# A transposed down-projection, six row buffers and a ScalarE copy in the last stage of an attention and gated-MLP kernel

## The chip, the cores and the metric

The kernel runs on one core of one Trainium2 chip. The time is the device time of that core in microseconds, as the median of several runs. The engines named here are PE (TensorE, matrix products), ACT (ScalarE, activations), DVE (VectorE), POOL (GpSimd) and SP (SyncE, which issues nearly all DMA transfers). Each engine works through its own queue of instructions in a fixed order, written out by the program when it is built.

## The reference

The input `x` has 2048 rows of 640 columns. It is normalized, and two branches read the result: attention with 32 heads of 20 columns, and a gated MLP of width 1728. Their results are combined.

```python
xn = _layernorm(x, axis=-1)
# A: q, k, v = xn @ wqkv, 32 heads of 20
scores = jnp.einsum("bhqd,bhkd->bhqk", q, k) * scale
p = _softmax(scores, axis=-1)
o = jnp.einsum("bhqk,bhkd->bhqd", p, v)
s = o @ wo
# B
h = _sigmoid(xn @ w_gate) * (xn @ w_up)
g = _silu(h @ w_down)
return x + s * g
```

## The kernel before

**Blocks.** The 32 heads form 8 groups of 4, and the 2048 queries form 4 chunks of 512, so there are 32 blocks (group, chunk). A block has 64 score tiles (4 heads by 16 tiles of 128 keys), each of 128 keys by 512 queries: 2048 in all. PE computes a score tile into a bank of PSUM. Two double banks, `scA0` and `scA1`, take two tiles each; three spare banks, `bk0` to `bk2`, take single tiles and the results of all other products. The four heads of a group occupy four strips of 32 rows of the array, so several score tiles run side by side (L900).

**Exponentials.** ScalarE takes most tiles out as exps, two at a time from a double bank (`pt<-scA`, 1024 columns) or one from a spare bank (`px<-bk`, 512 columns). The others go to VectorE, which makes an integer with the bits of a rough power of two (`iv`, L1336) and improves it in three passes over four tiles (`pb`, L1030, L1033, L1036). PE multiplies the results with `v` into one bank, `oacc` (L937). After each block VectorE copies `oacc` out (`norm_a`), and the denominators go through DRAM and back: SP stores `ld`, loads `lt`, VectorE takes reciprocals (`norm_b`), SP stores `rd` and loads `rl`, GpSimd multiplies, and SP puts the heads into `oU`.

**The MLP** fills PE between the scores. For each chunk of 512 rows there are 14 tiles of 128 columns of gate and up (`mk_gu`): ScalarE takes a tanh, VectorE a product, and `hT` holds the result with the MLP's columns on the partitions. Then comes the down-projection (`mk_down`): eight items per chunk, one for each 128 rows and each half of the 640 output columns, with 14 steps of four matmuls 320 columns wide. `hT` is the stationary operand, so rows come out on the partitions. ScalarE takes a tanh of 320 columns (`td`), VectorE a product (`gqs`), and SP stores it in `gq_dram` in fp32. The last chunk's product stays in SBUF (`gql`).

**Output.** Near the end `mk_out` multiplies `oU` with `wo` for each 128 rows and half of the columns, VectorE multiplies with the row of `gq_dram` that `load_out` has read back (`otmp`, L796), and GpSimd (L805) or, from row tile 8 on, VectorE (L814) adds `x`. Row buffers lie in the no longer needed part of `xnT`: three of them.

**The last stage** (`chain`, L1135 on) handles the last block and the last four row tiles. Most of their output products are formed early (`early`, L1057). When the last exp is multiplied, `oacc` is copied out in halves, transposed by PE, scaled and transposed back (`e_on` to `e_o`); `e_late` adds the last products (L1061). Four results of 512 columns (`mains`) lie in `bk0`, `bk1` and the halves of `scA1`; the last 128 columns of the four tiles lie in two banks (`rest`). VectorE multiplies them with `gql` (`t_main` L1107, `t_rest` L1113); GpSimd adds `x` for the first two tiles (L1110, L1117), VectorE for the last two (L1117, L1121); `t_out` stores.

**The order** of PE, ACT, DVE and POOL is written by a planner, the loop at the end of the kernel. It advances a clock in steps of 0.02 us with an assumed duration for every instruction and picks, for each engine that is free, the next work. PE chooses between score tiles (F), products with `v` (PV) and other items (M). Other items are held to a pace, at most `LEAD` us ahead of it; `M_ORD`, `DORD` and `XORD` set in which order the spare banks are tried for items, for VectorE's tiles and for ScalarE's extra tiles. GpSimd adds are placed by `beat` beside a VectorE instruction that reads PSUM, or all at once by `flush`. SP's order follows from when the planner's clock reaches each transfer.

Of the kernel before, what the change touches and what calls it, by code (L numbers as in the profile page):

```python
# [18 lines left out]
P = 128  # L19
# [11 lines left out]
URGENT, ROUNDS, HOLD, SLACK, LEAD, LAG, D_LAST, D_LAST_END = 0.2, 6, 0.0, 0.0, 40.0, 2.0, 20, 20  # L31
M_ORD, WAIT3, FALL, M_END = 1, 0.2, 1, 2.0
NPT, NPX, NPB, NIV = 12, 5, 3, 3
DVE_ADD = 8
XMAX, DQ, DORD, XORD, STARVE = 2, 1.4, 2, 0, 0.3
# [17 lines left out]
def kernel(  # L53
# [41 lines left out]
    gq_dram = dram.tile([S, D], FP32, name="gq_dram", tag="gqd", bufs=1)  # L95
# [352 lines left out]
    LATE, T_LT, T_OU, T_L2, T_RL = 1.0, 9.0, 1.5, 4.5, 5.6  # L448
# [216 lines left out]
    def mk_gu(c, kf, at):  # L665
# [20 lines left out]
        def th():  # L686
            st["t"] = w2.tile([P, QC], BF16, tag="tnh", bufs=2, name="tnh")
            act_imm(st["t"][0:fs, :], st["g"][0:fs, :], ACT.Tanh, 0.5)
# [8 lines left out]
        def th2():  # L697
            st["t"] = w2.tile([P, QC], BF16, tag="tnh", bufs=2, name="tnh")
            act_imm(st["t"][fs:P, :], st["g"][0:fs, :], ACT.Tanh, 0.5)
# [14 lines left out]
    def gq_last(t4):  # L714
        if len(gq_l) == t4 // 2:
            w = w2.tile([P, 2, KD, 2 * P], BF16, tag="wgu", bufs=2, name="gql")
            gq_l.append(w.rearrange("p i k f -> p (i k f)").bitcast(FP32))
        return gq_l[t4 // 2][:, t4 % 2 * D:(t4 % 2 + 1) * D]

    def mk_down(c, t4, h, at):  # L720
        st = {}
        tt = 4 * c + t4
# [4 lines left out]
        def mm(kf):  # L727
            cols(st["ps"][:, 0:HD], hT[:, kf, t4 * P:(t4 + 1) * P], wd[:, kf, h * HD:(h + 1) * HD],
                 kf == 0, kf == NFT - 1)

        def th():
            st["td"] = w2.tile([P, HD], BF16, tag="td", bufs=2, name="td")
            act_imm(st["td"], st["ps"][:, 0:HD], ACT.Tanh, 0.25)

        def ev():
            if c == NQC - 1:
                return nc.vector.scalar_tensor_tensor(out=gq_last(t4)[:, h * HD:(h + 1) * HD], in0=st["td"], scalar=1.0,
                                                      in1=st["ps"][:, 0:HD], op0=ALU.add, op1=ALU.mult)
            flush("o")
            gqs = w2.tile([P, HD], FP32, tag="gqs", bufs=3, name="gqs")  # L740
            ins = nc.vector.scalar_tensor_tensor(out=gqs, in0=st["td"], scalar=1.0, in1=st["ps"][:, 0:HD],
                                                 op0=ALU.add, op1=ALU.mult)
            nc.sync.dma_start(out=gq_dram[tt * P:(tt + 1) * P, h * HD:(h + 1) * HD], in_=gqs)
            return ins
        return Item([("PE", alloc, [(0.14, lambda kf=kf: mm(kf)) for kf in range(NFT)]),
                     ("ACT", 0.32, th), ("DVE", 0.40, ev, "free", mark("d", c, t4, h))], at, pre=[("h", c, kf) for kf in range(NFT)])
# [17 lines left out]

    def load_out(tt):
        if tt in out_tiles:
            return
        o2 = xfl[:, tt % 3 * KD * QC:tt % 3 * KD * QC + 3 * D]
        flush("o")
        out_tiles[tt] = (o2[:, 0:D], o2[:, D:3 * D].bitcast(FP32))  # L770
# [3 lines left out]
    def mk_out(tt, h, at):  # L774
        st = {}

        def alloc():
            if h == 0:
                load_out(tt)
                if (tt + 1) % 4:  # L780
                    load_out(tt + 1)
# [6 lines left out]
        def ev():  # L788
# [6 lines left out]
            tmp = w2.tile([P, 2 * HD], BF16, tag="gqs", bufs=3, name="otmp")[:, 0:HD]  # L795
# [16 lines left out]
        def add():  # L812
            xr = out_tiles[tt][0][:, h * HD:(h + 1) * HD]
            ins = nc.vector.tensor_tensor(out=xr, in0=st["tmp"], in1=xr, op=ALU.add)  # L814
            if h == 1:
# [4 lines left out]
                    pre=[("d", tt // 4, t4, i) for t4 in range(4) for i in range(2)] + [("h", 2, kf) for kf in range(NFT)] + (  # L820
# [4 lines left out]
    for c in range(NQC):  # L825
        for kf in range(NFT):
            glu.append(lambda at, c=c, kf=kf: mk_gu(c, kf, at))
        for h in range(2):
            for t4 in range(4):
                glu.append(lambda at, c=c, t4=t4, h=h: [mk_down(c, t4, h, at)])  # L830
# [271 lines left out]
    tmps = [hfl[:, t4 * 512:(t4 + 1) * 512] for t4 in range(4)]  # L1102
    tmp = hfl[:, 4 * 512:4 * 512 + 4 * EX].rearrange("p (t e) -> p t e", e=EX)
    xg = xl.rearrange("p (t u) -> p t u", u=D)

    def t_main(t4):
        nc.vector.scalar_tensor_tensor(out=tmps[t4], in0=mains[t4], scalar=0.25, in1=gq_last(t4)[:, 0:512],  # L1107
                                       op0=ALU.mult, op1=ALU.mult)
        if t4 < 2:
            nc.gpsimd.tensor_tensor(out=tail[t4][:, 0:512], in0=tmps[t4], in1=tail[t4][:, 0:512], op=ALU.add)  # L1110

    def t_rest(i):
        nc.vector.scalar_tensor_tensor(out=tmp[:, 2 * i:2 * i + 2, :],  # L1113
                                       in0=rest[i][:, 0:2 * EX].rearrange("p (t e) -> p t e", e=EX),
                                       scalar=0.25, in1=gq_l[i].rearrange("p (t u) -> p t u", u=D)[:, :, 512:D],
                                       op0=ALU.mult, op1=ALU.mult)
        (nc.vector if i else nc.gpsimd).tensor_tensor(out=xg[:, 2 * i:2 * i + 2, 512:D], in0=tmp[:, 2 * i:2 * i + 2, :],  # L1117
                                                      in1=xg[:, 2 * i:2 * i + 2, 512:D], op=ALU.add)

    def t_last(t4):  # L1120
        nc.vector.tensor_tensor(out=tail[t4][:, 0:512], in0=tmps[t4], in1=tail[t4][:, 0:512], op=ALU.add)  # L1121

    def t_out(t4):
        r = slice(4 * (NQC - 1) * P + t4 * P, 4 * (NQC - 1) * P + (t4 + 1) * P)
        eng = nc.sync if t4 % 2 == 0 else nc.scalar
        eng.dma_start(out=out2[r, :], in_=tail[t4])

    def t_done(i):
        t_rest(i)
        for t4 in (2 * i, 2 * i + 1):  # L1130
            if i:
                t_last(t4)
# [8 lines left out]
             ("DVE", 0.63, lambda: t_main(0), (10,)), ("DVE", 0.63, lambda: t_main(1), (10,)),  # L1141
# [397 lines left out]
```

## Time and profile before

| | us |
|---|---|
| median of 3 runs (801.88 to 803.19) | 802.37 |
| the profiled execution, its own time | 803.29 |
| its span, first to last instruction | 801.6 |

| engine | busy, us | share of the span | instructions |
|---|---|---|---|
| PE | 779.8 | 97% | 10465 |
| ACT | 781.8 | 98% | 992 |
| DVE | 770.1 | 96% | 1246 |
| POOL | 96.4 | 12% | 203 |

| group | count | mean of one, ns |
|---|---|---|
| ACT exp of two tiles, `pt` | 703 | 1192 |
| ACT exp of one tile, `px` | 137 | 762 |
| ACT tanh of the down-projection, `td` | 32 | 618 |
| DVE `iv` | 499 | 683 |
| DVE product of the down-projection, `gqs` and `gql` | 32 | 483, 475 |
| PE down-projection matmuls, 128x320 | 1792 | 302 |

The mean of one counts from an instruction's start to its end. Neighbours overlap on an engine, so what an instruction costs its engine is the distance to the next start, where the next one is ready. The DMA engines are busy for about a quarter of the time.

### The profile page before, as it was taken

The numbers are of one execution on the slowest core, as the hardware profiler recorded it, in microseconds if no ns is written. First come the engines' busy times: TensorE is split into PE (matmuls) and PEld (weight loads), VectorE is DVE, ScalarE is ACT, GpSimd is POOL, SyncE is SP. The second block draws the span as 40 slices with busy tenths as digits, with TensorE's granted clock in tenths as the row PEclk, the third lists the DMA queues.
The fourth block names the chain that finished last, engine by engine and source line by source line (L and its number), as shares of the span: only waits on it lengthen the run. The fifth ranks groups of instructions, "written<-read, shape, count | busy, mean of one in ns | idle before, by whom it ended". The sixth has DMA issues, their size and how long they took to land.

```text
span 801.6 us, 25384 instructions
## 1 busy us (share of the span) xinstructions
PE 779.8 (97%) x10465; PEld 284.4 (35%) x10465; DVE 770.1 (96%) x1246; ACT 781.8 (98%) x992; POOL 96.4 (12%) x203
## 2 busy tenths in 40 slices
PE   8899999999999999999999999999999999999997
PEld 5523333333433323334332332333333233333332
DVE  7798999999999999989999999999999999999997
ACT  8799999999999999999999999999999999999994
POOL 7200000000000000000000000000000100502302
PEclk9999999999999999999999999999999999999999
DMA  5441212223122223222113232222311332331421
GB/s 162 132 131 49 69 40 73 66 67 81 47 62 67 73 72 100 53 60 65 53 46 89 58 87 73 73 81 62 98 36 61 91 89 53 102 107 23 141 70 55
DMA packets 91851, 60.47 MB, mean 75 GB/s; under 512 B 34891, under 2 KB 85627, under 8 KB 91735
## 3 DMA queue, kind: packets, MB, share of 16 engines
q1 hardware_dynamic: 91447, 58.52, 26.1%
q8 instruction: 82, 1.34, 0.7%
q14 instruction: 34, 0.28, 0.1%
q10 hardware_dynamic: 288, 0.33, 0.1%
HBM read 45.18 MB, written 11.09 MB: 70 GB/s over the span
## 4 chain that ended last, share of the span: by engine, by line
PE 45%; ACT 41%; DVE 7%; issue 5%; DMA 1%; SPq 0%; POOL 0%; DVEq 0%; ACTq 0%; POOLq 0%
ACT pt L83 33%; PE bk L474 18%; PE scA L900 14%; PE oacc L937 9%; ACT px L83 4%; DVE iv L1336 2%; ACT tnh L83 2%; DVE pb L1036 1%; ACT td L83 1%; PE bk L900 1%; DVE pb L1033 1%; PE tp L293 1%; DVE pb L1030 0%; DMA lt<-ld 0%; DMA ld<-on 0%
## 5 line engine op out<-in xcount | busy, mean ns | idle before, releaser
L83 ACT ACTIVATE pt<-scA 128x1024 bf16<-128x1024 f32 (+1 forms) x709 | 708.7, 1188 | 0.7 <-PE bk L900 0.3
L1336 DVE TENSOR_SCALAR iv<-bk 128x512 int16<-128x512 f32 x499 | 332.2, 683 | 12.1 <-PE bk L900 9.6
L900 PE MATMUL scA<-q,kT 32*128 32x512 bf16 x1412 | 275.8, 382 | 8.8 <-ACT pt L83 3.3
L900 PE MATMUL bk<-q,kT 32*128 32x512 bf16 x636 | 207.3, 383 | 0.2 <-DVE iv L1336 0.2
L900 PEld LDWEIGHTS <-kT 32*128 32x128 bf16 x2048 | 88.4, 91 | 262.4 <-issue 251.1
L937 PE MATMUL oacc<-pt,v 128*21 128x512 bf16 x1412 | 178.5, 381 | 0.7 <-ACT pt L83 0.7
L937 PE MATMUL oacc<-pb,v 128*21 128x512 bf16 x998 | 160.8, 382 | 0.0
L474 PE MATMUL bk<-xnT,wgu 128*32 128x512 bf16 x2160 | 157.3, 383 | 0.5 <-DVE iv L1336 0.2
L1036 DVE TENSOR_TENSOR pb<-iv,pb 128x2048 bf16<-128x2048 bf16 (+1 forms) x125 | 151.8, 1214 | 0.7
L990 POOL TENSOR_TENSOR on_bf<-on,rl 128x128 bf16<-128x128 f32 x116 | 54.3, 472 | 626.8 <-DVE iv L1336 189.1
L83 ACT ACTIVATE px<-bk 128x512 bf16<-128x512 f32 x137 | 102.1, 762 | 1.7 <-POOL hT L1178 1.6
L474 PE MATMUL bk<-wd,hT 128*32 128x320 bf16 x1792 | 87.0, 302 | 0.1
L1030 DVE TENSOR_SCALAR pb<-iv 128x2048 int16<-128x2048 int16 (+1 forms) x125 | 86.0, 688 | 0.4
L1033 DVE TENSOR_SCALAR pb<-iv 128x2048 int16<-128x2048 int16 (+1 forms) x125 | 85.9, 688 | 0.0
L937 PEld LDWEIGHTS <-v 128*21 128x21 bf16 x2547 | 53.6, 91 | 76.2 <-issue 53.6
L474 PEld LDWEIGHTS <-wgu 128*32 128x32 bf16 x2160 | 44.5, 95 | 64.3 <-issue 46.3
L474 PEld LDWEIGHTS <-hT 128*32 128x32 bf16 x1792 | 37.5, 95 | 38.2 <-issue 32.7
L474 PE MATMUL bk<-xnT,wu 128*32 128x512 bf16 x640 | 48.5, 383 | 0.6 <-DVE iv L1336 0.2
L937 PE MATMUL oacc<-px,v 128*21 128x512 bf16 x137 | 47.0, 381 | 0.0
L83 ACT ACTIVATE tnh<-bk 128x512 bf16<-128x512 f32 (+1 forms) x56 | 43.4, 776 | 0.1
L691 DVE SCALAR_TENSOR_TENSOR hT<-tnh,bk 128x512 bf16<-128x512 bf16 x52 | 35.4, 680 | 1.0 <-PE bk L900 0.3
L655 PE MATMUL bk<-wv,xnT 128*128 128x160 bf16 x280 | 29.4, 235 | 0.6 <-ACT px L83 0.6
(120 smaller groups left out, 406.2 us busy)
## 6 DMA issues: line engine op xcount, KB each, us to landing
rl<-rd SPq DMA_DIRECT2D x124, 64.0 KB
wgu<-in_B_w_gate_dram SPq DMA_DIRECT2D x24, 320.0 KB
wgu<-in_B_w_up_dram SPq DMA_DIRECT2D x24, 320.0 KB
gq_dram<-gqs SPq DMA_DIRECT2D x24, 160.0 KB
xnT<-gq_dram SPq DMA_DIRECT2D x12, 320.0 KB
xt<-in_A_x_dram SPq DMA_DIRECT2D x16, 160.0 KB
xnT<-in_A_x_dram SPq DMA_DIRECT2D x16, 160.0 KB
out_dram<-xnT SPq DMA_DIRECT2D x14, 160.0 KB
```

The lines of the kernel that those rows point to most:

```text
L83: return nc.scalar.add_instruction(mybir.InstActivation(func=func, name=nc.get_next_instruction_name(), engine=ENG.Activation, ins=[nc.sca ...
L293: nc.tensor.transpose(out=tps[k][:, kd, :], in_=xns[k][:, kd * P:(kd + 1) * P], identity=ident)
L474: nc.tensor.matmul(out[j:j + 32, :], lhsT=lhsT[:, j:j + 32], rhs=rhs, start=start, stop=stop, tile_position=(0, j), skip_group_check=True)
L655: nc.tensor.matmul(st["ps"][:, i * 2 * GC:(i + 1) * 2 * GC], lhsT=xn_tok(tts[i], kd), rhs=wvs[pr][:, kd, :], start=(kd == 0), stop=(kd == ...
L691: return nc.vector.scalar_tensor_tensor(out=hT[0:fs, kf, :], in0=st["t"][0:fs, :], scalar=1.0, in1=st["u"][0:fs, :], op0=ALU.add, op1=ALU. ...
L900: nc.tensor.matmul(dst, lhsT=kTs[gc_of(b)[0] % 2][32 * j:32 * j + 32, kt * P:(kt + 1) * P], rhs=qts[b % 3][32 * j:32 * j + 32, :], start=T ...
L937: nc.tensor.matmul(oacc[32 * j:32 * j + DH + 1, :], lhsT=lhsT, rhs=u["src"], start=first, stop=last, tile_position=(0, 32 * j), skip_group ...
L990: ins = nc.gpsimd.tensor_tensor(out=on_bf[:, cs], in0=on[:, cs], in1=rl[:, cs], op=ALU.mult)
L1030: ins = nc.vector.tensor_scalar(out=pb[:, 0, :, :].bitcast(I16), in0=iv, scalar1=0x7F80, scalar2=1, op0=ALU.bitwise_and, op1=ALU.bitwise_or)
L1033: ins = nc.vector.tensor_scalar(out=pb[:, 1, :, :].bitcast(I16), in0=iv, scalar1=0x007F, scalar2=0x3F00, op0=ALU.bitwise_and, op1=ALU.bitw ...
L1036: ins = nc.vector.tensor_tensor(out=pb[:, 1, :, :], in0=iv.bitcast(BF16), in1=pb[:, 1, :, :], op=ALU.mult)
L1336: beat(nc.vector.tensor_scalar(out=d["iv"][:, j, :], in0=bank[bk], scalar1=B_OFF, scalar2=0.0, op0=ALU.add, op1=ALU.max))
```

## The change

The down-projection swaps its operands. `wd` becomes the stationary one and `hT` the moving one, so an item is one tile of 128 output columns for all 512 rows of the chunk: five items per chunk, matmuls 512 wide. Output columns now lie on the partitions, so SP transposes each product with a DMA into `g4`, and a second transfer stores that in `gq_dram`, which is now bf16. For the last chunk the transpose writes straight into `gql`. `gqs` and `g4` have one buffer each. The planner issues the transpose 0.8 us after VectorE's product starts (`T_GT`) and the store 5.8 us after it (`T_GO`).

With bf16 rows, six row buffers fit where three were, and `load_out` is called up to `AHEAD` = 4 row tiles ahead.

In the last stage ScalarE copies one bank of each half out of PSUM, scaled by 0.25 (`t_copy`), and VectorE's product for these two banks reads SBUF alone. The add of the first half's last 128 columns moves from GpSimd to VectorE. VectorE adds each of the last two tiles in one instruction of 640 columns. Three of the four stores go through SP.

Four of the planner's settings change too: `LEAD` from 40 to 30, `M_ORD` from 1 to 0, `DORD` from 2 to 0 and `XORD` from 0 to 1. The tanh buffers become three and are shared with the down-projection.

```diff
-URGENT, ROUNDS, HOLD, SLACK, LEAD, LAG, D_LAST, D_LAST_END = 0.2, 6, 0.0, 0.0, 40.0, 2.0, 20, 20
-M_ORD, WAIT3, FALL, M_END = 1, 0.2, 1, 2.0
+URGENT, ROUNDS, HOLD, SLACK, LEAD, LAG, D_LAST, D_LAST_END = 0.2, 6, 0.0, 0.0, 30.0, 2.0, 20, 20
+M_ORD, WAIT3, FALL, M_END = 0, 0.2, 1, 2.0
...
-XMAX, DQ, DORD, XORD, STARVE = 2, 1.4, 2, 0, 0.3
+AHEAD = 4
+XMAX, DQ, DORD, XORD, STARVE = 2, 1.4, 0, 1, 0.3
...
-    gq_dram = dram.tile([S, D], FP32, name="gq_dram", tag="gqd", bufs=1)
+    gq_dram = dram.tile([S, D], BF16, name="gq_dram", tag="gqd", bufs=1)
...
-    def mk_down(c, t4, h, at):
+    def mk_down(c, e, at):
...
-            cols(st["ps"][:, 0:HD], hT[:, kf, t4 * P:(t4 + 1) * P], wd[:, kf, h * HD:(h + 1) * HD],
-                 kf == 0, kf == NFT - 1)
+            cols(st["ps"], wd[:, kf, e * P:(e + 1) * P], hT[:, kf, :], kf == 0, kf == NFT - 1)
...
-            st["td"] = w2.tile([P, HD], BF16, tag="td", bufs=2, name="td")
-            act_imm(st["td"], st["ps"][:, 0:HD], ACT.Tanh, 0.25)
+            st["td"] = w2.tile([P, QC], BF16, tag="tnh", bufs=3, name="td")
+            act_imm(st["td"], st["ps"], ACT.Tanh, 0.25)
...
-            nc.sync.dma_start(out=gq_dram[tt * P:(tt + 1) * P, h * HD:(h + 1) * HD], in_=gqs)
+            es = slice(e * P, (e + 1) * P)
+            g4 = w2.tile([P, 4, P], BF16, tag="g4", bufs=1, name="g4") if c < NQC - 1 else gq_last()[:, :, es]
+            timed.append((now + T_GT, lambda: nc.sync.dma_start_transpose(out=g4, in_=gqs)))
+            if c < NQC - 1:
+                timed.append((now + T_GO, lambda: nc.sync.dma_start(
+                    out=gq_dram[c * QC:(c + 1) * QC, es].rearrange("(t p) u -> p t u", p=P), in_=g4)))
...
-        o2 = xfl[:, tt % 3 * KD * QC:tt % 3 * KD * QC + 3 * D]
+        o2 = xfl[:, tt % 6 * 2 * D:(tt % 6 + 1) * 2 * D]
...
-            if h == 0:
-                load_out(tt)
-                if (tt + 1) % 4:
-                    load_out(tt + 1)
+            load_out(tt)
+            n = len(out_tiles)
+            if n < NOUT and n <= tt + AHEAD and (n < 6 or ("o", n - 6, 1) in ev_at) and all(
+                    ("d", n // 4, i) in ev_at for i in range(KD)):
+                load_out(n)
...
+    def t_add(eng, t4, a, b):
+        eng.tensor_tensor(out=tail[t4][:, a:b], in0=tmp[:, t4, a:b], in1=tail[t4][:, a:b], op=ALU.add)
+
+    def t_copy(t4):
+        act_imm(tmp[:, t4, 0:512], mains[t4], ACT.Copy, 0.25)
+
     def t_main(t4):
-        nc.vector.scalar_tensor_tensor(out=tmps[t4], in0=mains[t4], scalar=0.25, in1=gq_last(t4)[:, 0:512],
+        if t4 % 2:
+            nc.vector.tensor_tensor(out=tmp[:, t4, 0:512], in0=tmp[:, t4, 0:512], in1=gq_last()[:, t4, 0:512], op=ALU.mult)
+        else:
+            nc.vector.scalar_tensor_tensor(out=tmp[:, t4, 0:512], in0=mains[t4], scalar=0.25, in1=gq_last()[:, t4, 0:512],
+                                           op0=ALU.mult, op1=ALU.mult)
+        if t4 < 2:
+            t_add(nc.gpsimd, t4, 0, 512)
...
+        if not i:
+            nc.vector.tensor_tensor(out=xg[:, 0:2, 512:D], in0=tmp[:, 0:2, 512:D], in1=xg[:, 0:2, 512:D], op=ALU.add)
...
-        eng = nc.sync if t4 % 2 == 0 else nc.scalar
+        eng = nc.sync if t4 < 3 else nc.scalar
...
             if i:
-                t_last(t4)
+                t_add(nc.vector, t4, 0, D)
             t_out(t4)
```

## The prediction, made before the result was known

> **What bounds the kernel now.** The busy shares come first: PE 97%, DVE 96% and ACT 98% of the span, so the page alone does not say which of the three sets the pace. The profile cut into stretches of time does.
>
> ```profile
> 100.00:300.00 200.00, 197.32 (x2656) 68.05 (x2654) 197.39 (x316) 199.89 (x251) 16.32 (x36) 1.00 0.24 65
> 300.00:500.00 200.00, 196.90 (x2651) 68.20 (x2652) 194.18 (x304) 199.89 (x252) 14.39 (x32) 1.00 0.25 68
> 500.00:700.00 200.00, 197.07 (x2698) 70.47 (x2691) 197.63 (x311) 199.76 (x247) 24.02 (x48) 1.00 0.26 73
> 786.00:801.60 15.60, 9.93 (x81) 4.22 (x77) 9.62 (x21) 4.57 (x8) 2.88 (x3) 0.92 0.19 67
> ```
>
> The columns are PE, its weight loads, DVE, ACT and POOL. From 100 to 700 us ScalarE is busy for 599.5 of 600 us, PE for 591.3 and DVE for 589.2: ScalarE leads, with the other two close. Only after 786 us does it stand idle. Its timeline then shows what one instruction costs when the next follows at once.
>
> ```profile
> 399.07 3.99 ACT L83 ACTIVATE pt<-scA 128x1024 bf16<-128x1024 f32 x4
> 402.70 0.69 ACT L83 ACTIVATE td<-bk 128x320 bf16<-128x320 f32 x1
> 403.02 6.79 ACT L83 ACTIVATE pt<-scA 128x1024 bf16<-128x1024 f32 x7
> 409.43 0.71 ACT L83 ACTIVATE td<-bk 128x320 bf16<-128x320 f32 x1
> ```
>
> A 128x320 tanh takes 0.69 us but holds the engine for 0.32 (402.70 to 403.02). Seven exps of 1024 columns take 6.41, or 0.92 each. Over all starts from 40 to 786 us, a 1024-column exp has a median distance of 0.904 to the next start, and a 512-column one 0.477. What lies above these values is ScalarE waiting for scores under cover of its own latency, which "busy" hides: 13.0 us in 693 such exps. So 13 us is about all that a smoother order could win in the middle.
>
> The end is the other place. The timeline of the last 20 us:
>
> ```profile
> 781.27 1.85 POOL L995 TENSOR_TENSOR on_bf<-on,rl 128x512 bf16<-128x512 f32 x1 [18.24 <-DMA rl<-rd]
> 781.90 1.40 DVE L814 TENSOR_TENSOR xnT<-otmp,xnT 128x320 bf16<-128x320 bf16 x1
> ...
> 793.80 1.29 DVE L1107 SCALAR_TENSOR_TENSOR hT<-bk,gql 128x512 bf16<-128x512 f32 x2 [0.55 <-PE bk L1061]
> ...
> 794.64 2.26 POOL L1110 TENSOR_TENSOR xnT<-hT,xnT 128x512 bf16<-128x512 bf16 x2 [11.52 <-DVE hT L1107]
> ...
> 795.01 0.41 DVE L1113 SCALAR_TENSOR_TENSOR hT<-bk,gql 128x256 bf16<-128x256 f32 x1
> ...
> 795.42 1.29 DVE L1107 SCALAR_TENSOR_TENSOR hT<-scA,gql 128x512 bf16<-128x512 f32 x2
> ...
> 796.86 0.66 POOL L1117 TENSOR_TENSOR xnT<-hT,xnT 128x256 bf16<-128x256 bf16 x1
> 797.08 0.59 DVE L1117 TENSOR_TENSOR xnT<-hT,xnT 128x256 bf16<-128x256 bf16 x1
> ```
>
> VectorE works without a gap from 793.80 to 798.34 (the end of the last adds, L1121), then the last rows go out. And two pairs of these lines show VectorE and GpSimd excluding each other. The L814 add starts at 781.90 while GpSimd is at work until 783.12, and ends at 783.30: 1.40 us, against a median of 0.316 for its line. The L1117 add ends at 797.67, 0.15 us after GpSimd's 797.52. But the L1107 products, whose first input lies in PSUM, keep their 0.68 us right beside GpSimd's L1110. So a VectorE tensor_tensor on two SBUF inputs waits for a running GpSimd add; a product that reads PSUM does not.
>
> **The change, part by part.**
>
> *ScalarE's work.* From the two instruction orders: 32 tanhs of 320 columns become 20 of 512 (-32x0.317 + 20x0.477 = -0.60 us); two-bank exps 703 to 701 (-1.81), one-bank exps of a spare bank 137 to 140 (+1.43), half-filled exps 6 to 7 (+0.48). VectorE still takes 499 of the 2048 score tiles. Sum: **-0.5 us**, all on the engine that bounds.
>
> *PE and VectorE.* Down-projection streams 448 groups of 320 columns at 0.136 us before and 280 of 512 at 0.216 after: 60.9 against 60.5. Runs of it between score fills fall from 135 to 114; each entry and return costs some 0.10 us over the bare stream (0.32 against 0.216), so PE gains about 2 us. VectorE: -32x0.397 + 20x0.597 = -0.8. Neither bounds the middle; taken as nothing, and the cover is ScalarE's 599.5 of 600 us.
>
> *The order.* LEAD, the bank choices and the longer items rearrange PE from the first block on. What matters is how much PE work stands between two score fills against the exps that must bridge it. I price each stretch by the rows above (0.216 per 512-column stream, 0.21 for leaving and returning to scores) and subtract ScalarE's work of the same fill. In the trace of before, stretches where PE has over 0.15 us more than ScalarE cost ScalarE 0.07 us each on average, those within 0.05 cost 0.01. There are 111 such stretches before and 124 after; by that count the stalls go from 14.5 to 15.0 us (this count takes in the first exps). But they also follow one another more often: runs of four with over 0.2 us too much go from 36 to 57, and a straight-line fit of the measured stalls on single stretches and on runs of two and three gives 17.2. So +0.5 to +2.7; I take the middle, **+1.6 us**, as the two counts are equally near to the rows. The far bounds: all stretches at the quiet 0.01 (709x0.010 = 7 us) is -7.5; twice today's stalls is +14.5.
>
> *Transposes, stores, buffers.* SP issues 20 transposes and 15 stores for 24 stores, 11 more at 0.33 to 0.4 us; they stand between the loads of softmax denominators, weights and q. A store behind a transpose holds SP until it lands. No row has a transpose. Nearest is a round trip over DRAM: ld issued 397.62, lt (waiting for it) 399.35, 1.7 us. There is one gqs buffer, so VectorE's next product waits until the transpose has read it, with all later VectorE work queued behind. By ScalarE's order two tanhs are at least 6.9 us apart (7.3 to 11.4 mostly), which leaves 6.2 after the product's 0.7. So: nothing, unless a transpose takes over 6.2 us. [...] Loading rows ahead removes 9.0 us in which SP waited for otmp and 7.8 for output stores, but L796, the reader of those rows, has 0.0 us of idle before it: nothing.
>
> *Between last exp and end stage.* Before, the last exp ends at 789.83 and VectorE's first copy starts at 790.91, 1.08 later, as PE still has rows of oacc and early products to do. The new order leaves five PV matmuls, some 0.7 us: **-0.35** (0 to -0.4).
>
> *The end stage.* ScalarE's copy starts at 794.02 (its matmul ends at 793.98) and takes some 0.58 (the 512-column L174 from idle: 575 ns), to 794.60. The new SBUF product of bank 1 can start near 794.64, exactly when GpSimd's first add starts (794.638). If GpSimd is first, the product waits to 795.79 and ends at 796.06; GpSimd's second add runs 796.2 to 797.35; the add that moved from GpSimd to VectorE waits for it, to 797.5; then 0.61 (bank 2), 0.41 (bank 3), 0.33 (rest) and two adds of some 0.43 end at 799.7: +1.35. If VectorE is first, GpSimd runs 795.06 to 796.15 and 796.15 to 797.26, holds the moved add and the bank 3 product, and the end is 798.8: +0.45. Without any exclusion it is 797.9: -0.4. I take **+0.9**, the middle of the two with exclusion, which both pairs of rows show. [...]
>
> **Sum:** -0.54 + 1.6 - 0.35 + 0.9 = +1.6 us. The profiled execution took 803.29 us (span 801.57 and 1.72 around it), 0.92 above the median 802.37. So 804.9 against its own time and **804.0** against the median.
>
> **Rivals.**
> 1. *The new order stalls ScalarE less* (ends faster). Longer items change banks less often and free PE 2 us; if that counts more than the bunching, the stalls fall halfway to the quiet value, -3.75, and the sum is -3.7: 798.6. For it: PE shrinks. Against: stretches and runs over the limit grow. The other terms sum to 0.0, so it decides once the 13.0 us of waiting fall below 11.4 (-1.6).
> 2. *No exclusion in the end stage*, stalls +0.5: -0.54 + 0.5 - 0.35 - 0.4 = -0.8: 801.6. Against it stand L814 and L1117.
> 3. *Transposes are slow.* At 9 us the twenty products wait 13.9 us in all (each gap short of 9.7 us added up); if half reaches the end, +7 on the forecast: 811. Against: 1.7 us for a plain round trip.
>
> **How the numbers follow.** Some 0.2% (1.6 us) is what a measurement can tell from no change. Forecast 0.50 (its own range, with both ends of the stall and end-stage terms, 802.4 to 805.5), rival 1 0.26, rival 2 0.10, rival 3 0.14. The forecast lies at the 0.2% bound, and its stall term is open upwards: of its 0.50 I give 0.29 to slower and 0.21 to same. Faster: 0.24 of rival 1 and 0.01 of rival 2, 0.25; same: 0.21 + 0.02 + 0.09 = 0.32; slower: 0.29 + 0.14 = 0.43. The range leaves out the lower half of rival 1 and the slow end of rival 3: 799.0 to 808.5.
>
> **What would show it.** ScalarE's distances above 0.904 should sum to 13.5 to 16 us from 40 to 786. In the end stage the product of bank 1 or the moved add should last over 0.8 us beside a GpSimd add, and the last VectorE add should end 4.9 to 5.9 us after the first product's start (4.54 before). The product into gqs should start without waiting for a DMA. The prediction is wrong if the stalls fall under 11.4 us, if these adds keep 0.3 to 0.5 us, or if VectorE waits for transposes.

## The result, and the profile after

| | kernel before | changed kernel |
|---|---|---|
| median of 6 runs, us | 802.37 (801.88 to 803.24) | 805.72 (804.65 to 806.05) |
| ratio, with its 95% interval | | 1.0037 (1.0027 to 1.0047) |
| the profiled execution, us | 803.29 | 806.05 |
| its span, us | 801.57 | 804.35 |

The changed kernel is slower by 0.27 to 0.47%, more than the 0.2% that a measurement can tell from no change. The time lies in the predicted range, 1.7 us above the forecast and 0.2 above the 802.4 to 805.5 that the prediction gave for its own terms.

The spans of the two profiles can be compared piece by piece. "Work" counts each activation from the first exp on at the undisturbed distance of its form (0.904, 0.477, 0.317 us); "stalls" are what lies above it.

| piece | before | after | difference |
|---|---|---|---|
| start to first exp | 30.98 | 30.04 | -0.94 |
| ScalarE's work, first exp to start of last exp | 743.44 | 742.51 | -0.93 |
| stalls before 700 us | 12.33 | 12.65 | +0.32 |
| stalls from 700 us on | 2.33 | 5.20 | +2.87 |
| the last exp | 0.76 | 1.15 | +0.39 |
| its end to VectorE's first copy | 1.07 | 0.74 | -0.33 |
| copy to the first product of the last stage | 2.89 | 3.02 | +0.13 |
| first product to the end of VectorE's last add | 4.54 | 5.90 | +1.36 |
| the rest | 3.23 | 3.14 | -0.09 |
| sum | 801.57 | 804.35 | +2.78 |

The first row goes with PE's clock at the start, not with a stage of the change. In nine of the thirteen profiles of this document the trace's record of the full clock begins at 4.2 to 6.0 us (with one stretch of 3.4 us at 0.50 behind it), and the first exp comes at 29.9 to 30.3. In the other four (before, and experiments 6, 8 and 9) it begins at 13.8 to 14.1; up to there the 128x256 filler matmuls (`scrap`) last 0.42 us instead of 0.27, and the first exp comes at 30.8 to 31.0. Two of these four have the changed code, so the code alone does not set it; whether the kernel before can also start early, no profile shows. Two rows make the loss: the stalls from 700 us on, and the last stage.

The profile of the changed kernel cut into the same stretches (PE, its weight loads, DVE, ACT, POOL, then the granted clock):

```profile
100.00:300.00 200.00, 196.50 (x2496) 63.69 (x2488) 198.48 (x314) 199.95 (x247) 18.54 (x36) 1.00 0.25 65
300.00:500.00 200.00, 195.99 (x2510) 64.05 (x2510) 196.48 (x306) 199.86 (x251) 15.25 (x32) 1.00 0.27 70
500.00:700.00 200.00, 197.12 (x2515) 64.34 (x2511) 194.64 (x304) 199.80 (x245) 22.13 (x45) 1.00 0.28 73
788.30:804.40 16.10, 8.36 (x64) 3.70 (x63) 8.12 (x16) 5.18 (x8) 2.30 (x2) 0.89 0.12 45
```

From 100 to 700 us ScalarE leads as before, 599.6 of 600 us. So the middle is not where the time went.

**The event at 730 us.** The timeline of SP's queue (start, duration, transfer) in the changed kernel, and then the same transfers of the same block in the kernel before:

```profile
724.89 0.76 SPq L1022 DMA_DIRECT2D oU<-on_bf  x1
725.76 1.23 SPq L740 DMA_TRANSPOSE gql<-gqs  x1
727.04 0.75 SPq L1022 DMA_DIRECT2D oU<-on_bf  x1
727.89 0.53 SPq L974 DMA_DIRECT2D ld<-on  x1
728.48 1.50 SPq L1022 DMA_DIRECT2D oU<-on_bf  x2
730.08 0.42 SPq L976 DMA_DIRECT2D lt<-ld  x1
```

```profile
723.98 2.27 SPq L1020 DMA_DIRECT2D oU<-on_bf  x3
726.36 0.53 SPq L972 DMA_DIRECT2D ld<-on  x1
726.93 0.73 SPq L1020 DMA_DIRECT2D oU<-on_bf  x1
728.06 0.35 SPq L974 DMA_DIRECT2D lt<-ld  x1
```

`norm_a` issues the store `ld` and the load `lt` one after the other, yet transfers to `oU` stand between them on SP: the order on SP is not simply that in which the planner's clock reaches each transfer, as the description of the kernel before has it. In the changed kernel a transpose stands ahead of `ld` and holds the queue for 1.23 us, and two transfers instead of one stand between `ld` and `lt`. VectorE's copy (L972), whose result `ld` stores, came only 0.16 us later than before (723.54 against 723.38), but `lt` is issued 2.02 us later. Of these, 0.91 are there before the first transfer shown: GpSimd's four multiplies of the previous block, which release the `oU` transfers, end at 724.86 instead of 723.96. The other 1.11 are on the queue: from the first of the four `oU` transfers to `lt` it takes 5.19 us with the transpose among them, and took 4.08 without. So the transpose makes about half of the delay, and the new order of the engines the rest. Now VectorE, then ScalarE, in the changed kernel (start, duration, what ended the idle time before):

```profile
723.54 0.68 DVE L972 COPY on<-oacc 128x512 f32<-128x512 f32 x1
...
727.80 1.28 DVE L1345 TENSOR_SCALAR iv<-bk 128x512 int16<-128x512 f32 x2
731.77 0.25 DVE L982 RECIPROCAL rt<-lt 128x16 f32<-128x16 f32 x1 [2.69 <-DMA lt<-ld]
...
733.75 0.68 DVE L1345 TENSOR_SCALAR iv<-bk 128x512 int16<-128x512 f32 x1
```

```profile
736.17 1.02 ACT L84 ACTIVATE pt<-scA 128x1024 bf16<-128x1024 f32 x1 [2.00 <-PE bk L902]
737.69 1.02 ACT L84 ACTIVATE pt<-scA 128x1024 bf16<-128x1024 f32 x1 [0.49 <-PE bk L902]
739.20 2.07 ACT L84 ACTIVATE pt<-scA 128x1024 bf16<-128x1024 f32 x2 [0.48 <-PE bk L902]
```

VectorE stands 2.69 us in front of its reciprocal. In the kernel before it had stood 0.79 at this place, and 0.66 one block later:

```profile
729.62 0.25 DVE L980 RECIPROCAL rt<-lt 128x16 f32<-128x16 f32 x1 [0.79 <-DMA lt<-ld]
...
753.64 0.25 DVE L980 RECIPROCAL rt<-lt 128x16 f32<-128x16 f32 x1 [0.66 <-DMA lt<-ld]
```

Behind the reciprocal in the changed kernel's queue, after two passes over `pb`, is the `iv` that empties a spare bank; PE, whose next matmul needs that bank, stands for 2.19 us; and ScalarE runs out of scores. The stretches around it show a second loss:

```profile
732.00:734.40 2.40, 0.29 (x3) 0.09 (x1) 2.37 (x5) 2.17 (x3) 0.00 (x0) 1.00 0.04 3
734.40:736.90 2.50, 2.41 (x31) 0.71 (x30) 2.47 (x6) 0.73 (x1) 0.00 (x0) 0.82 0.45 136
736.90:739.70 2.80, 2.80 (x26) 0.47 (x22) 1.88 (x4) 1.82 (x3) 0.00 (x0) 0.55 0.18 25
```

After the gap PE's granted clock falls to half: in slices of 0.2 us it is 0.53 at 736.0 and 0.50 from 736.2 to 739.4, some 3.4 us in all, and score matmuls there last 0.61 us instead of 0.39. The two shorter waits of ScalarE, 0.49 and 0.48, lie there. The three waits make 2.97 us. Counted by the distance of starts, as in the table, they are 2.41, 0.61 and 0.60 us, together 3.62 against 0.36 at this place before: the whole rise of 2.87 from 700 us on, and more.

**The last stage** of the changed kernel, VectorE, GpSimd and ScalarE in order of time:

```profile
795.31 0.69 DVE L1117 SCALAR_TENSOR_TENSOR hT<-bk,gql 128x512 bf16<-128x512 f32 x1 [0.62 <-PE bk L1063]
...
796.14 1.15 POOL L1108 TENSOR_TENSOR xnT<-hT,xnT 128x512 bf16<-128x512 bf16 x1 [12.22 <-ACT hT L84]
796.16 1.42 DVE L1115 TENSOR_TENSOR hT<-hT,gql 128x512 bf16<-128x512 bf16 x1 [0.15 <-ACT hT L84]
...
797.72 1.15 POOL L1108 TENSOR_TENSOR xnT<-hT,xnT 128x512 bf16<-128x512 bf16 x1 [0.42 <-DVE hT L1115]
797.94 1.07 DVE L1128 TENSOR_TENSOR xnT<-hT,xnT 128x256 bf16<-128x256 bf16 x1
...
799.54 0.41 DVE L1115 TENSOR_TENSOR hT<-hT,gql 128x512 bf16<-128x512 bf16 x1
```

GpSimd starts 0.02 us ahead of VectorE's product of two SBUF inputs, and that product ends 0.29 us after GpSimd's add; the same product without GpSimd beside it takes 0.41. The moved add (L1128) again lasts until GpSimd is done: it ends at 799.01, GpSimd's second add at 798.87.

### The profile page after: what moved, and what is told of

It is laid out like the page before. It is cut to its first block, busy times and chain, and to the rows that moved or that the text cites. A ratio compares the mean times of both kernels' runs of the same rounds, so it can differ in the third digit from the quotient of the medians.

```text
span 804.3 us, 24012 instructions
## 1 busy us (share of the span) xinstructions
PE 773.9 (96%) x9788; PEld 263.5 (33%) x9793; DVE 770.0 (96%) x1234; ACT 782.7 (97%) x984; POOL 100.0 (12%) x202
## 4 chain that ended last, share of the span: by engine, by line
ACT 54%; PE 21%; DVE 14%; issue 9%; DMA 1%; SPq 1%; POOL 0%; DVEq 0%; ACTq 0%; POOLq 0%
ACT pt L84 43%; PE bk L475 8%; PE scA L902 6%; ACT px L84 6%; DVE iv L1345 6%; PE oacc L939 4%; ACT tnh L84 3%; DVE pb L1038 2%; DVE pb L1032 1%; DVE pb L1035 1%; ACT td L84 1%; DVE hT L692 1%; PE tp L294 1%; DMA xt<-in_A_x_dram 0%; PE psk L144 0%
## 5 line engine op out<-in xcount | busy, mean ns | idle before, releaser
L84 ACT ACTIVATE pt<-scA 128x1024 bf16<-128x1024 f32 x708 | 698.8, 1162 | 3.4 <-PE bk L902 3.0
L902 PE MATMUL bk<-q,kT 32*128 32x512 bf16 x639 | 203.1, 384 | 0.2
L939 PE MATMUL oacc<-pt,v 128*21 128x512 bf16 x1409 | 185.4, 382 | 0.9 <-ACT pt L84 0.8
L902 PEld LDWEIGHTS <-kT 32*128 32x128 bf16 x2048 | 85.9, 91 | 289.2 <-issue 279.1
L475 PE MATMUL bk<-xnT,wgu 128*32 128x512 bf16 x2160 | 159.1, 383 | 0.8
L84 ACT ACTIVATE px<-bk 128x512 bf16<-128x512 f32 x140 | 100.4, 730 | 1.7 <-POOL hT L1187 1.6
L475 PE MATMUL bk<-hT,wd 128*32 128x512 bf16 x1120 | 83.2, 386 | 2.7 <-DVE iv L1345 2.4
L84 ACT ACTIVATE tnh<-bk 128x512 bf16<-128x512 f32 (+1 forms) x56 | 41.5, 741 | 0.1
L475 PEld LDWEIGHTS <-wd 128*32 128x32 bf16 x1120 | 20.7, 95 | 35.8 <-issue 29.5
```

The costliest lines, as they stand in the source:

```text
L84: return nc.scalar.add_instruction(mybir.InstActivation(func=func, name=nc.get_next_instruction_name(), engine=ENG.Activation, ins=[nc.sca ...
L475: nc.tensor.matmul(out[j:j + 32, :], lhsT=lhsT[:, j:j + 32], rhs=rhs, start=start, stop=stop, tile_position=(0, j), skip_group_check=True)
L902: nc.tensor.matmul(dst, lhsT=kTs[gc_of(b)[0] % 2][32 * j:32 * j + 32, kt * P:(kt + 1) * P], rhs=qts[b % 3][32 * j:32 * j + 32, :], start=T ...
L939: nc.tensor.matmul(oacc[32 * j:32 * j + DH + 1, :], lhsT=lhsT, rhs=u["src"], start=first, stop=last, tile_position=(0, 32 * j), skip_group ...
```

## The experiments

Each median is of 11 executions (4 in experiment 6), beside runs of the kernel before on the same chip (802.52, 802.56 and 802.33 us in the three groups). Waits, gaps and stalls are of one profiled execution each.

**1. The last stage of before.** All products read PSUM, no ScalarE copies, GpSimd adds the first half's last columns again, and the stores alternate between SP and ScalarE's queue again; all else as changed.

```diff
-        if t4 % 2:
-            nc.vector.tensor_tensor(out=tmp[:, t4, 0:512], in0=tmp[:, t4, 0:512], ...)
-        else:
-            nc.vector.scalar_tensor_tensor(out=tmp[:, t4, 0:512], in0=mains[t4], ...)
+        nc.vector.scalar_tensor_tensor(out=tmp[:, t4, 0:512], in0=mains[t4], ...)
...
-            nc.vector.tensor_tensor(out=xg[:, 0:2, 512:D], ...)
+            nc.gpsimd.tensor_tensor(out=xg[:, 0:2, 512:D], ...)
...
-             ("ACT", 0.55, lambda: t_copy(1), (10,)),
```

> The changed kernel with the last stage of before: no ScalarE copies, all four products read PSUM, GpSimd adds the first half's last 128 columns again (the two 640-column adds of the second half stay). Exclusion of GpSimd and VectorE as the cause: nothing on VectorE waits for GpSimd before the second half, and from the first product's start to the end of the last add it takes 4.0 to 4.6 us instead of 5.9, so the time falls by 1.3 to 1.9 us, to about 804. Rival, the stage is long because the copies or PE come late: it also gets shorter, but no VectorE add or SBUF product lasts over 0.8 us in either kernel. Rival, the stage is not on the path that ends last: no change, 805.7.

Measured 804.06 us (803.28 to 804.80), ratio 1.0019 (1.0010 to 1.0028). Its last stage:

```profile
795.19 1.29 DVE L1114 SCALAR_TENSOR_TENSOR hT<-bk,gql 128x512 bf16<-128x512 f32 x2 [0.61 <-PE bk L1063]
796.02 2.26 POOL L1108 TENSOR_TENSOR xnT<-hT,xnT 128x512 bf16<-128x512 bf16 x2 [12.40 <-DVE hT L1114]
796.39 0.42 DVE L1120 SCALAR_TENSOR_TENSOR hT<-bk,gql 128x256 bf16<-128x256 f32 x1
796.73 1.28 DVE L1114 SCALAR_TENSOR_TENSOR hT<-scA,gql 128x512 bf16<-128x512 f32 x2
```

Products that read PSUM run undisturbed right through GpSimd's 2.26 us (1.28 for the last two, where one alone takes 0.68 in experiment 2); the stage takes 4.46 us instead of 5.90.

**2. The same work without GpSimd.** The ScalarE copies and the SBUF products stay, but VectorE does all adds.

```diff
-        if t4 < 2:
-            t_add(nc.gpsimd, t4, 0, 512)
...
-            if i:
-                t_add(nc.vector, t4, 0, D)
+            t_add(nc.vector, t4, 0, D)
```

> The changed kernel with its ScalarE copies, but GpSimd adds nothing in the last stage: VectorE adds all four row tiles, 640 columns each. Exclusion: the SBUF product of bank 1 keeps 0.41 us, the stage takes about 4.7 us although VectorE has more to do, and the time falls by about 1.2 us, to 804.5. Without exclusion VectorE has two adds of 0.43 us more and one of 0.25 less, and the time rises by 0.6, to 806.3.

Measured 804.41 us (802.97 to 805.49), ratio 1.0018 (1.0010 to 1.0027). Two of its lines:

```profile
796.23 0.42 DVE L1115 TENSOR_TENSOR hT<-hT,gql 128x512 bf16<-128x512 bf16 x1 [0.15 <-ACT hT L84]
...
797.03 0.89 DVE L1108 TENSOR_TENSOR xnT<-hT,xnT 128x640 bf16<-128x640 bf16 x2
```

The product takes 0.42 us, and the stage 4.73 although VectorE now has two adds of 640 columns in place of one of 2x128. So the 1.4 us are the exclusion, not the amount of VectorE's work: giving the second engine nothing was better than sharing in this form; sharing with products that read PSUM (experiment 1, 4.46) is better still. In both runs the event at 730 us is as in the changed kernel (waits for `lt` of 2.65 and 2.88, clock 0.50), which shows that the two losses stand apart.

**3. Plain copies for the last chunk's transposes.** Each of the five `gql` transposes becomes an ordinary transfer at the same place of the queue. The gate of the last 512 rows then stays untransposed, so this part of the output is another.

```diff
-            timed.append((now + T_GT, lambda: nc.sync.dma_start_transpose(out=g4, in_=gqs)))
+            timed.append((now + T_GT, lambda: (nc.sync.dma_start_transpose(out=g4, in_=gqs) if c < NQC - 1 else
+                                               nc.sync.dma_start(out=g4, in_=gqs.rearrange("p (t u) -> p t u", u=P)))))
```

> The changed kernel with the last chunk's five transposes replaced by plain copies of the same bytes (the last chunk's gate is therefore not transposed); the order on every engine and on SP is the same. SP queue as the cause of the 2.7 us in which VectorE waits for lt at 729 to 732 us: SP holds 1.25 us for a transpose and some 0.4 for a copy, so lt lands 0.8 to 0.9 us sooner, VectorE waits about 1.8 us, ScalarE's waiting between 700 and 760 us falls from 4.4 to 2.5 to 3.5, and the time by 0.9 to 2.5 us, to 803.2 to 804.8. Bunched PE work as the cause: the waiting and the time stay, 805.7.

Measured 804.06 us (803.77 to 806.21), ratio 1.0024 (1.0015 to 1.0033). On SP, and then on VectorE:

```profile
725.90 0.67 SPq L741 DMA_DIRECT2D gql<-gqs  x1
...
729.69 0.43 SPq L977 DMA_DIRECT2D lt<-ld  x1
```

```profile
731.37 0.25 DVE L983 RECIPROCAL rt<-lt 128x16 f32<-128x16 f32 x1 [2.16 <-DMA lt<-ld]
```

The plain copy holds SP for 0.67 instead of 1.23 us, and VectorE's wait shrinks by about that, 0.53. PE's gap is 1.66 instead of 2.19, and the clock stays at 1.00. Stalls from 700 us fall from 5.20 to 2.99. By the distance of starts the event costs 1.88 instead of 3.62: the first stall is shorter by the 0.53 us of the queue, and the two behind it, which lay in the slow clock, are gone (1.2). So half a microsecond on SP's queue was worth 1.7 us on ScalarE. The wait that is left, more than the 1.8 that was expected, has the causes that are left: the copy itself, the `oU` transfers around `ld` and `lt`, and their later start.

**4. Later reciprocals.** The last three blocks' reciprocals are due 7.0 us after the copy instead of 4.5, so VectorE does other work while `lt` is on its way.

```diff
-    LATE, T_LT, T_OU, T_L2, T_RL, T_GT, T_GO = 1.0, 9.0, 1.5, 4.5, 5.6, 0.8, 5.8
+    LATE, T_LT, T_OU, T_L2, T_RL, T_GT, T_GO = 1.0, 9.0, 1.5, 7.0, 5.6, 0.8, 5.8
```

> The changed kernel with T_L2 7.0 instead of 4.5: the planner lets VectorE ask for lt 2.5 us later in blocks 28 to 30; the order up to there is the same. Late lt as the cause: VectorE waits under 0.5 us for lt, PE has no gap of 2 us and keeps its full clock, ScalarE's waiting between 700 and 760 us falls from 4.4 to about 1.5, and the time by 2.4 to 3.6 us, to about 802.7. Bunched PE work as the cause: no wait for lt, but the time stays within 1 us, 804.7 to 806.7.

Measured 804.33 us (803.23 to 805.82), ratio 1.0024 (1.0015 to 1.0033). The wait is 0.23 us, PE has no gap there, and the stalls of 700 to 760 us fall from 4.36 to 1.08. But 1.5 us come back after 760 us:

```profile
758.00:760.00 2.00, 1.24 (x12) 0.30 (x12) 2.00 (x3) 2.00 (x4) 0.24 (x1) 1.00 0.30 88
760.00:762.00 2.00, 1.09 (x13) 0.34 (x11) 1.97 (x3) 1.95 (x3) 1.02 (x1) 1.00 0.00 0
762.00:764.00 2.00, 0.99 (x13) 0.25 (x12) 2.00 (x5) 1.55 (x3) 0.00 (x0) 1.00 0.13 31
...
768.00:770.00 2.00, 2.00 (x23) 0.40 (x15) 1.54 (x4) 1.63 (x2) 0.00 (x0) 0.53 0.00 0
```

A changed due time changes the planner's order after it. Now PE has three gaps of 0.9 to 1.0 us within 7 us (none of them longer than 1.02), and again the clock falls, to 0.53.

**5. The settings undone.** The changed kernel with the four planner settings of before.

```diff
+URGENT, ROUNDS, HOLD, SLACK, LEAD, LAG, D_LAST, D_LAST_END = 0.2, 6, 0.0, 0.0, 40.0, 2.0, 20, 20
+M_ORD, WAIT3, FALL, M_END = 1, 0.2, 1, 2.0
...
+XMAX, DQ, DORD, XORD, STARVE = 2, 1.4, 2, 0, 0.3
```

> The changed kernel with the four planner settings of the kernel before (LEAD 40, M_ORD 1, DORD 2, XORD 0); the transposed down-projection, the row buffers and the last stage stay. By the order, ScalarE has 707 two-bank exps, 10 half-filled ones and 125 of a spare bank, against 701, 7 and 140: 0.3 us less work. SP-queue theory (the middle's loss is a load of denominators that stands behind a transpose and the head transfers, the settings themselves are worth little): the head transfers now come before the store ld, but one transpose still stands between ld and lt, so VectorE's longest wait for lt is 0.5 to 2 us; stalls before 700 us stay at 12.3 to 13, those of 700 to 760 us are 2 to 3.5; end stage 5.8 to 5.9 us as in the changed kernel; 803.8 to 805.2. Order theory (the settings bunch the PE work between score fills, and that is the loss): stalls before 700 us fall well below 12.3, and the time comes down to 803 or less although the end stage is unchanged.

Measured 803.26 us (803.00 to 805.40), ratio 1.0013 (1.0005 to 1.0022). Stalls before 700 us are 12.41 (12.65 with the new settings): the settings are worth nothing there. The longest wait for `lt` is 1.69 us, PE's gap 0.90, the clock stays at 1.00, and the stalls from 700 us on are 3.80. The last stage is 5.91 us.

Yet the median falls by 2.5 us, to below the 803.8 to 805.2 of the SP-queue theory and near the 803 of the order theory, whose sign (fewer stalls before 700 us) is missing. Of the 2.06 us between the two profiles, 1.40 lie in the stalls from 700 us on, 0.24 in those before, and 0.51 in the last exp, which is a half-filled one. So much of the loss hangs on the settings, and the part from 700 us on comes through the order on SP. Near 730 us VectorE now waits 0.18; the 1.69 are at 751, where no transpose is near. There a load of `x` into a row buffer (L773) stands between `ld` and `lt`:

```profile
745.73 0.55 SPq L974 DMA_DIRECT2D ld<-on  x1
748.96 0.33 SPq L773 DMA_DIRECT2D xnT<-in_A_x_dram  x1
749.34 0.42 SPq L976 DMA_DIRECT2D lt<-ld  x1
```

SP stands still for 2.62 us in front of this load, until an earlier store of an output row (`out_dram<-xnT`) has landed, and `lt` stands behind it.

**6. The settings alone,** on the kernel before (the reverse of that diff).

> The kernel before with the four new planner settings alone (LEAD 30, M_ORD 0, DORD 0, XORD 1). No transposes, old last stage. By the order, ScalarE has 712 two-bank exps, 5 half-filled ones and 123 of a spare bank, against 703, 6 and 137: +1.0 us of work, and its last exp is a full one. SP-queue theory: stalls stay at 14 to 15.5 us, last stage 4.5 us, no VectorE wait for lt over 1.5 us: 803.0 to 804.0, all of it ScalarE's work. Order theory: stalls before 700 us rise from 12.3 to 14 or more: 805 and above. If the changed kernel's first exp, 0.94 us earlier than before, comes from the settings, it is near 30.0 us here too, otherwise near 31.

Measured 811.03 us (809.75 to 811.30), ratio 1.0100 (1.0086 to 1.0114). The SP-queue theory's numbers all failed. The order theory's came out (13.98 us of stalls before 700 us, and over 805), but what happens before 700 us is the smaller part of the loss. Stalls before 700 us rise by 1.65, of which one wait at 354 us makes 1.4; those from 700 us on rise from 2.33 to 6.57, and the end (start of the last exp to the last add) takes 10.9 us instead of 9.3. There is no transpose in this kernel, and yet it has the same event, and the largest. SP, VectorE, and the stretch behind it:

```profile
752.08 2.84 SPq L771 DMA_DIRECT2D xnT<-in_A_x_dram  x2
755.00 0.56 SPq L972 DMA_DIRECT2D ld<-on  x1
755.66 0.39 SPq L772 DMA_DIRECT2D xnT<-gq_dram  x1
756.81 0.33 SPq L974 DMA_DIRECT2D lt<-ld  x1
```

```profile
758.89 0.25 DVE L980 RECIPROCAL rt<-lt 128x16 f32<-128x16 f32 x1 [3.20 <-DMA lt<-ld]
```

```profile
762.00:764.00 2.00, 2.00 (x27) 0.57 (x19) 2.00 (x4) 1.56 (x3) 0.49 (x2) 0.50 0.69 183
```

Two loads of `x` stand ahead of `ld`, whose data had been ready since 751.3, and the second of them holds SP for 2.11 us until a store of an output row has landed, as in experiment 5. So it is not the transpose as such that matters, but whatever stands on SP's queue around `ld` and `lt`.

**7. Both repairs,** the last stage of experiment 1 and reciprocals 7.0 us after the copy; and **8.** the same with 6.0.

> Both repairs of the changed kernel together: the last stage of the kernel before (all products from PSUM, no ScalarE copies, GpSimd adds the first half's last columns) and the last three reciprocals due 7.0 us after the copy instead of 4.5. If the two losses are independent: the last stage at 4.4 to 4.6 us, VectorE's wait for lt under 0.5 us, no drop of the granted clock at 730 to 740 us, stalls 15 to 16.5 us as with the later reciprocals alone, so 804.3 - 1.4 = 802.9, between 802.3 and 803.4. If something else holds the end (the last stores, say), the last stage is shorter but the time stays at 804.

> The same with the reciprocals due 6.0 us after the copy. By the order the last two transposes now both come between the loads rl and the head transfers, outside of the way from ld to lt, and the last exp is a half-filled one (0.43 us less than a full one). SP-queue theory: VectorE still waits some 1.2 us for lt (2.7 less the 1.5 us by which the reciprocal comes later), stalls in 700 to 760 us of 2 to 3.5; last stage 4.4 to 4.6; 802.3 to 803.5. If only the full removal of that wait counts, it is slower than the variant with 7.0 us by about 1 us.

Measured: 804.00 us (802.72 to 805.31) with 7.0, which is 1.1 above what was expected, and 802.36 us (801.68 to 802.98) with 6.0, ratio 0.9994 (0.9985 to 1.0004). The last stage is 4.48 and 4.47 us in both. With 7.0 the three gaps of PE and the clock of 0.50 at 766 us are there as in experiment 4. With 6.0 the wait for `lt` is 0.78, PE has no gap over 0.90, the clock is 1.00 throughout, and the stalls from 700 us on are 1.58, less than in the kernel before; the last exp is a half-filled one, as there. The whole loss of the change is undone, and nothing is won: the profile's 0.85 us less from first to last exp is within what the medians leave open.

**9. The transposed form alone:** experiment 1 with the old settings too. **10** and **11** add reciprocals 5.5 and 6.0 us after the copy.

> The transposed down-projection and the six row buffers alone: the four planner settings and the last stage are those of the kernel before. By the order, ScalarE has 707 two-bank exps, 10 half-filled ones, 125 of a spare bank and 20 tanhs of 512 columns, 0.8 us of work less than the kernel before. Independent losses: the last stage at 4.4 to 4.6 us instead of 5.9, all else as in the changed kernel with the old settings (VectorE waits some 1.7 us for lt near 750 us, stalls near 16 us): 803.3 - 1.4 = 801.9, between 801.3 and 802.6. If the transposed form itself costs time (bunched matmuls, transposes), it stays at 803 or more.

> The same with the last three reciprocals due 5.5 us after the copy instead of 4.5. SP-queue theory: the wait for lt near 750 us shrinks by about 1 us to 0.7, the stalls from 700 us fall from 3.8 to 2 to 3 us: 801 to 801.9, and with that 0.1 to 0.2% under the kernel before. If these waits do not matter, it is the same as with 4.5 us to 0.3.

> The same with 6.0 us. The wait for lt near 750 us is 0 to 0.3 us; but by the order the last exp is a full one (0.43 us longer). SP-queue theory: stalls from 700 us at 1.6 to 3, 801 to 802. If the later blocks' order takes the gain back, as it did in the changed kernel with 7.0 us (1.5 us of new stalls after 760 us), 802 to 803.

Measured: 804.00 us (802.04 to 805.65), 802.58 (801.63 to 803.38) and 802.08 (801.23 to 803.07), ratios 1.0017 (1.0007 to 1.0027), 0.9999 (0.9990 to 1.0008) and 0.9996 (0.9987 to 1.0005). Number 9 was expected at 801.9 and came out no faster than experiment 5, of which it should have been a repair (804.00 and 803.26; the intervals of their ratios overlap). That is the time of its rival, 803 or more, but not by bunched matmuls or transposes. Its profiled run, at 805.59 us one of the slowest of its eleven, shows the load of `x` again; SP stands 3.20 us in front of it instead of 2.62:

```profile
746.70 0.55 SPq L974 DMA_DIRECT2D ld<-on  x1
750.51 0.33 SPq L773 DMA_DIRECT2D xnT<-in_A_x_dram  x1
750.89 0.42 SPq L976 DMA_DIRECT2D lt<-ld  x1
```

```profile
752.83 0.25 DVE L982 RECIPROCAL rt<-lt 128x16 f32<-128x16 f32 x1 [2.30 <-DMA lt<-ld]
```

```profile
752.00:754.00 2.00, 0.69 (x13) 0.10 (x3) 1.17 (x2) 2.00 (x4) 0.00 (x0) 1.00 0.38 119
754.00:756.00 2.00, 1.79 (x18) 0.56 (x21) 2.00 (x5) 0.82 (x2) 0.53 (x2) 0.61 0.14 39
756.00:758.00 2.00, 2.00 (x23) 0.46 (x19) 1.61 (x2) 0.30 (x1) 0.76 (x2) 0.54 0.34 102
```

In the same place where experiment 5 waited 1.69 us with the clock at 1.00, this run waited 2.30 and lost the clock: 3.46 us of stalls around it, against 1.35. Its eleven times spread over 3.6 us; those of 8, 10 and 11, whose profiles show no drop, over 1.3 to 1.8. But experiment 5, without a drop, spreads over 2.4, and the changed kernel, with one, over 1.4, so the spread alone is no sign of it. In 10 and 11 the later due time also reorders SP's queue, and the same load waits some 0.8 us. The last stage is 5.03 us in 9, not 4.5: with the old settings PE still has eight early products (1.89 us) to form between the two halves, and VectorE waits 0.86 for the second.

The thirteen kernels together; the waits, gaps and clock (lowest over 2 us) are from 690 us on, each from its one profiled run:

| kernel | median, us | longest wait for lt | PE's longest gap | lowest clock | stalls from 700 us | last stage |
|---|---|---|---|---|---|---|
| before | 802.37 | 0.79 | 0.26 | 1.00 | 2.33 | 4.54 |
| changed | 805.72 | 2.69 | 2.19 | 0.50 | 5.20 | 5.90 |
| 1 old last stage | 804.06 | 2.65 | 2.15 | 0.50 | 4.94 | 4.46 |
| 2 no GpSimd at the end | 804.41 | 2.88 | 2.37 | 0.50 | 5.32 | 4.73 |
| 3 plain copies | 804.06 | 2.16 | 1.66 | 1.00 | 2.99 | 5.89 |
| 4 reciprocals 7.0 | 804.33 | 0.23 | 1.02 | 0.53 | 3.46 | 5.90 |
| 5 old settings | 803.26 | 1.69 | 0.90 | 1.00 | 3.80 | 5.91 |
| 6 settings alone | 811.03 | 3.20 | 2.71 | 0.50 | 6.57 | 5.10 |
| 7 = 1 and 7.0 | 804.00 | 0.18 | 1.02 | 0.50 | 3.08 | 4.48 |
| 8 = 1 and 6.0 | 802.36 | 0.78 | 0.90 | 1.00 | 1.58 | 4.47 |
| 9 = 1 and 5 | 804.00 | 2.30 | 1.52 | 0.54 | 5.27 | 5.03 |
| 10 = 9 and 5.5 | 802.58 | 0.94 | 0.63 | 1.00 | 3.05 | 5.04 |
| 11 = 9 and 6.0 | 802.08 | 1.02 | 0.63 | 1.00 | 3.09 | 4.89 |

Of the eight changed forms with a wait for `lt` over 1.5 us or three gaps in a row, none comes below 803.2; the three without (8, 10, 11) are all at the time of the kernel before.

## Why the prediction was right, and where it was wrong

- *ScalarE's work, -0.5.* Right: -0.93 up to the last exp and +0.39 for the last exp, which became a full one: -0.54. (The four terms of the prediction make -0.50; that its sum used -0.54 changes nothing.)
- *The order, +1.6 (0.5 to 2.7), by bunching of PE work.* Wrong in its mechanism, and too small. Stalls rose by 3.19 us, but only 0.32 of that lies before 700 us, although the new order differs from the first block on. The lower end of the two counts, +0.5, was the right one for bunching; experiment 5 bears that out, as the old settings leave the stalls before 700 us within 0.24. (In the kernel before, the same settings add 1.65 there, so this holds for the transposed form alone.) What the count of PE work could not see is that the settings also reorder SP's transfers; undoing them was worth 2.5 us in all.
- *Transposes, stores, buffers: "So: nothing, unless a transpose takes over 6.2 us".* This is the step that failed. It checked who waits for the transposes' result, and there the reading was right: the product into `gqs` waited for no DMA, only 0.6 us in all for a tanh. It did not ask who stands behind the transposes on SP's queue, although it noted that they "stand between the loads of softmax denominators". Those denominators have a reciprocal at a fixed due time and VectorE's whole queue behind them. The row that bore the warning was in the profile of before: VectorE already waited 0.79 and 0.66 us for `lt`, so there was no slack left for a transfer of over a microsecond. What the runs showed in its place is the event at 730: 2.87 us more stalls. The transpose is not all of it. It makes 1.11 of the 2.02 us by which `lt` is late, and a plain copy in its place (0.67 us on the queue instead of 1.23) took 1.7 us off; the other 0.91 are GpSimd's later multiplies, by the new order. So no run shows the 0 that the sum took for the transposes: on the queue one took 1.23 us where a plain copy took 0.67. The row buffers, which the prediction put at nothing because the reader of the rows never waits, have the same flaw: in experiments 5 and 9 it is their load of `x` that stands ahead of `lt`.
- *Between last exp and end stage, -0.35.* Right: -0.33.
- *The end stage, +0.9 (0.45 VectorE first, 1.35 GpSimd first).* The mechanism was right, and GpSimd was first: +1.36. The middle was a poor choice, since the tie had been worked out to within 0.002 us, and either order gives an end, not the middle.
- *Rival 1* (stalls fall) is out: they rose. *Rival 2* (no exclusion) is out: 1.42 against 0.41 us, and experiments 1 and 2 remove it in two ways. *Rival 3* (slow transposes) named one of the transfers at work, but with the wrong wait and too high a price.
- *What would show it.* The distances of 1024-column exps above 0.904 from 40 to 786 us sum to 15.0 us, inside the stated 13.5 to 16 (by the same 0.904 the kernel before has 12.3, not the 13.0 of the prediction), and the test was passed by another mechanism: a sum cannot tell many small stalls from one large one. The places of the stalls would have.

The sum came out as +1.6 and the profiles differ by 2.8, of which 0.9 less at the start goes with the clock there; the medians differ by 3.35. What the forecast lacked is the rise from 700 us on (2.9, all of it the event at 730) less the bunching it charged in vain (1.3 of its 1.6), and half a microsecond of the last stage. That the forecast came as near as 1.7 us is luck in part: the bunching stood in the sum for a loss that had another cause.

## What to carry to other kernels

A queue that issues transfers is an engine with an order: here a transpose held SP for 1.23 us, and `ld` and `lt` stood behind it. When an instruction is added to such a queue, list what stands behind, and follow the transfers with a due reader (here a store, a load and a reciprocal) to the engine that stands still. Look for readers that already wait a little (0.79 us here), because they have no slack; moving the reader back by 1 to 1.5 us was worth 1.4 to 1.9 us here (in part through the new order that came with it), and moving it by 2.5 broke the order elsewhere. A load into a buffer that waits for an earlier store blocks what stands behind it in the same way: such loads held SP for 2.11, 2.62 and 3.20 us here. And sum stalls by place before explaining them: here one event held as much as the whole rise.

## What was not expected of the hardware

**The clock after a short gap.** PE's granted clock fell to half for some 3.4 us after PE had stood still for 1.5 to 2.7 us once, or for 0.9 to 1.0 us three times within 7 us; after one gap of 1.66 (experiment 3) or 0.90 it did not. So the length of the gap alone does not decide: one of 1.52 us (number 9) was followed by a drop and one of 1.66 was not, and in experiment 4, where no gap was longer than 1.02, PE was still busy for 1.0 to 1.2 of each 2 us from 758 to 764 and for more after it, ahead of the drop. What does decide, no run here shows. In the changed kernel the drop made 0.97 of the 2.97 us, in number 9 the wait of 1.78.

**Two inputs in SBUF beside GpSimd.** A VectorE instruction of that kind does not become slower in proportion; in the rows here it ends after GpSimd's instruction, by 0.12 to 0.15 us less than its own length. The adds and products that take 0.29 to 0.41 us alone ended 0.14 to 0.29 us after it (0.41 became 1.42, and the add of 256 columns, 0.29 alone in experiment 6, lasted 1.07). A pass over `pb` in experiment 6 (L1036, 2048 columns, 1.21 us alone) lasted 2.18 and ended 1.08 us after GpSimd's 128x512 multiply.

**What a transpose costs the queue.** In the changed kernel a 128x512 transpose holds SP for 1.20 to 1.45 us (two of the twenty for 1.91 and 2.08), in experiment 3 a plain copy of the same data for 0.67 to 0.74, and in the kernel before a plain store of `gqs` to DRAM for 0.35 in the median. That it arrives in time was not in doubt here; the queue's time was the price.
